# Respacing ScalarE's shrink work and the transform steps around TensorE's products

## The chip, the cores and the metric

The kernel runs on one core of a Trainium2 chip. The metric is device time in microseconds (us) of one execution; lower is better. Before the change the median was 2817.23 us (2814.24 to 2818.3).

## The reference

Two blocks, joined by a reshape, all in f32. The first multiplies a spectrum by a filter; the second is a feed-forward block whose nonlinearity is x − tanh(x):

```python
def _attn_ref(x, filt_r, filt_i):                 # x: 8 x 3008 x 256
    Y = np.fft.rfft(x, axis=1) * (filt_r + 1j * filt_i)[None, :, :]
    return np.fft.irfft(Y, n=x.shape[1], axis=1)

def _moe_ref(x, w_in, w_out):                     # x: 24064 x 256, d_ff = 2048
    h = x @ w_in
    g = h - np.tanh(h)
    return g @ w_out
```

## The kernel before

TensorE does nearly all the arithmetic. The eight sequences are worked in five batches: a single one, three pairs, a single one (in the code `UNITS = [(0,), (1, 2), (3, 4), (5, 6), (7,)]`). A batch has groups of tokens (6, 12, 12, 12, 6), a group has four **units**; 192 units in all. A unit's code interleaves four streams: `up` (the first product of the feed-forward block, as seven block products, here called P1 to P7), `shrink` of the unit before (x − tanh x), `down` of the unit before that (the second product, into the banks `o`; both `d()` and `e()` take its next piece), and **transform steps**, `t(0)` to `t(4)`, which do the spectral work of the *next* batch. In the last batch the steps are empty.

The `up` part, with cuts. `X`, `Y`, `Z` are banks of PSUM. P1, P6, P7, P4 all go into X, so X must be copied out before the next of them starts:

```python
def up(U, d, e, s, t):
    ...
    steps_at = ([1, 2, 0, 1, 0, 1, 1, 0] if U > 1 else [0, 0, 1, 0, 2, 0, 1, 2])
    ...                                   # shrinks(k) does steps_at[k] steps of shrink
    mm(X, 1, True)                        # P1
    mm(Y, 2, True)                        # P2
    s1 = copied("s1")                     # ScalarE copies X
    t(0); d(); shrinks(0)
    V.tensor_add(h[:, 0, :, 0:w], Y, s1)  # VectorE reads Y
    e(); shrinks(1)
    t(1)                                  # second transform step
    mm(X, 6, False)                       # P6
    mm(Z, 5, True)                        # P5
    u2 = copied("u2")
    shrinks(2); d(); shrinks(3); e()
    t(2)                                  # third
    mm(X, 7, False)                       # P7
    u3 = copied("u3")
    V.tensor_add(h[:, 3, :, 0:w], Z, u3)
    shrinks(4); d(); shrinks(5); e()
    t(3)                                  # fourth
    mm(X, 4, False)                       # P4
    V.tensor_copy(h[:, 2, :, 0:w], X)     # VectorE copies X; the next unit's P1 waits for it
    shrinks(6); d(); e()
    t(4)
    mm(Z, 3, False)                       # P3
    V.tensor_add(h[:, 1, :, 0:w], Z, u2)
    shrinks(7)
```

(Joined with semicolons here to save lines.) The shrink works on two halves of a unit's `h`, first half 2, then half 0. Per half there are three activations on ScalarE and two operations on VectorE: turn (arctan), power (a square, with a sum), the product h·y, square, and end:

```python
def start(k):
    ACT.activation(y[k], ht[k], AF.Arctan, scale=S)                    # turn
    ACT.activation(y[k], y[k], AF.Square, accum_out=y_sums[...])       # power
def square(k):
    V.tensor_mul(ht[k], ht[k], y[k])                                   # the product
    ACT.activation(sq[k], y[k], AF.Square, bias=near_b, scale=A)       # square
def end(k):
    V.scalar_tensor_tensor(out=ht[k], in0=sq[k], scalar=K, in1=ht[k], ...)

start(2); yield; square(2); yield; end(2); yield
start(0); yield; square(0); yield; end(0)
combine(...)                              # GpSimd sums for the second product
```

One kind of transform step, called `pz` after its tile, ends in this chain over four engines; a `pe` step of the same or a later unit reads its `uv`:

```python
ACT.mul(zs[0:IM], pz[IM:128], -1.0)       # L443
ACT.copy(zs[IM:128], pz[0:IM])            # L444
V.tensor_mul(rows(uv), rows(pz), fr)      # L445
G.tensor_mul(rows(zs), rows(zs), fi)      # L446, GpSimd
G.tensor_add(uv, uv, zs)                  # L447, GpSimd
```

Of the kernel before, what the change touches and what calls it, by code (L numbers as in the profile page):

```python
# [48 lines left out]
def chunks_of(unit, size):  # L49
    n = steps_of(unit)  # L50
    return [(r, min(size, n - r)) for r in range(0, n, size)]
# [92 lines left out]
def kernel(  # L144
# [10 lines left out]
    V, G, ACT = nc.vector, nc.gpsimd, nc.scalar  # L155
# [20 lines left out]
    groups = [(p, c) for p, bs in enumerate(UNITS) for c in range(len(chunks_of(bs, CH)))]  # L176
# [346 lines left out]
    def combine(b, t, shared=False):  # L523
        G.tensor_sub(t[0], b[0][1], b[0][0])  # L524
        G.tensor_sub(t[1], b[1][1], t[0])  # L525
        (V if shared else G).tensor_sub(t[2], b[1][1], b[0][1])  # L526
        G.tensor_sub(t[3], t[1], b[1][0])  # L527
# [4 lines left out]
    def up(U, d, e, s, t):  # L532

        i, u = divmod(U, 4)
        b, tu, w = uts[i]
        rhs = [b[0][0], b[1][0], b[1][1], tu[:, 3, 0:w], tu[:, 0, 0:w], tu[:, 1, 0:w],
               tu[:, 2, 0:w]]
        banks = {k: ps.tile([128, 2, 256], F32, tag=k, bufs=1, name=k) for k in "xyz"}
        X, Y, Z = (banks[k][:, :, 0:w] for k in "xyz")
        h = dn.tile([128, 4, 2, 256], F32, tag="h", bufs=3, name="h")  # L540
        hs[U] = (h, w)

        def mm(bank, q, first):
            for k in range(2):
                nc.tensor.matmul(bank[:, k], wu[:, q - 1, (2 * u + k) * 128:(2 * u + k + 1) * 128],  # L545
                                 rhs[q - 1], start=(first and k == 0), stop=True,
                                 skip_group_check=True)

        def copied(tag):
            t = dn.tile([128, 2, 256], F32, tag=tag, bufs=1, name=tag)[:, :, 0:w]  # L550
            ACT.copy(t, X)  # L551
            return t




        steps_at = ([1, 2, 0, 1, 0, 1, 1, 0] if U > 1 else [0, 0, 1, 0, 2, 0, 1, 2])

        def shrinks(at):
            for _ in range(steps_at[at]):  # L560
                s()

        mm(X, 1, True)
        mm(Y, 2, True)
        s1 = copied("s1")
        t(0)
        d()
        shrinks(0)
        V.tensor_add(h[:, 0, :, 0:w], Y, s1)  # L569
        e()  # L570
        shrinks(1)
        t(1)
        mm(X, 6, False)
        mm(Z, 5, True)
        u2 = copied("u2")
        shrinks(2)
        d()
        shrinks(3)
        e()
        t(2)  # L580
        mm(X, 7, False)
        u3 = copied("u3")
        V.tensor_add(h[:, 3, :, 0:w], Z, u3)  # L583
        shrinks(4)
        d()
        shrinks(5)
        e()
        t(3)
        mm(X, 4, False)
        V.tensor_copy(h[:, 2, :, 0:w], X)  # L590
        shrinks(6)
        d()
        e()
        t(4)
        mm(Z, 3, False)
        V.tensor_add(h[:, 1, :, 0:w], Z, u2)
        shrinks(7)

    def shrink(U):

        h, w = hs.pop(U)
        ht = {k: h[:, k:k + 2].rearrange("p a b n -> p (a b) n")[:, :, 0:w] for k in (0, 2)}

        def tiles(tag, bufs):
            return dn.tile([128, 4, 256], F32, tag=tag, bufs=bufs, name=tag)[:, :, 0:w]

        y, sq = {}, {}

        def start(k):
            y[k] = tiles("y", 2)  # L610
            ACT.activation(y[k], ht[k], AF.Arctan, scale=S)  # L611
            ACT.activation(y[k], y[k], AF.Square,  # L612
                           accum_out=y_sums[:, 2 * U + k // 2:2 * U + k // 2 + 1])

        def square(k):
            sq[k] = tiles("sq", 1)
            V.tensor_mul(ht[k], ht[k], y[k])  # L617
            ACT.activation(sq[k], y[k], AF.Square, bias=near_b, scale=A)  # L618

        def end(k):  # L620
            V.scalar_tensor_tensor(out=ht[k], in0=sq[k], scalar=K, in1=ht[k],  # L621
                                   op0=ALU.add, op1=ALU.mult)

        start(2)
        yield
        square(2)
        yield
        end(2)
        yield
        start(0)  # L630
        yield
        square(0)
        yield
        end(0)
        t = dn.tile([128, 4, 2, 256], F32, tag="t", bufs=2, name="t")
        blocks = [[h[:, 2 * a + k, :, 0:w] for k in range(2)] for a in range(2)]
        combine(blocks, [t[:, k, :, 0:w] for k in range(4)], U + 1 == 4 * len(groups))
        gs[U] = (blocks, t, w)
        yield
# [64 lines left out]
    def store(i, o):  # L704


        p, c = groups[i]
        r, n = CHUNKS[p][c]
        ws_ = widths(p, c)
        total = sum(ws_)  # L710
        ot = dn.tile([128, 2, CH * 128], F32, tag="ot", bufs=1, name="ot")
        for h in range(2):
            V.transpose(ot[:, h, 0:total], o[:, h, 0:total])
        b = UNITS[p][0]
        if len(UNITS[p]) == 2:
            blocks = [(r + 32 * q * NR, n, 32 * q) for q in range(4)]
        else:
            blocks = [(r_h + 32 * q * NR, n_h, rows.start + 32 * q)
                      for _, rows, r_h, n_h in halves(p, r, n) for q in range(2)]
        for h in range(2):  # L720
            for k in range(4):
                for row, m, lo in blocks:
                    outs.append((
                        dram(out.tensor, (b * SEQ + row) * DM + h * 128 + 32 * k,
                             [[NR * DM, 32], [DM, m], [1, 32]]),
                        ot[32 * k:32 * k + 32, h, :].rearrange(
                            "p (j c) -> p j c", c=128)[:, 0:m, lo:lo + 32]))
# [26 lines left out]
    def store_some(n):  # L754
        for dst, src in outs[:n]:
            nc.sync.dma_start(dst, src)
        del outs[:n]
# [81 lines left out]
    with tc.tile_pool(name="tr", bufs=2) as tr, tc.manual_schedule():  # L839
        with tc.tile_pool(name="pro", bufs=1) as pro, \  # L840
# [136 lines left out]
            for j in range(NK // 2):  # L977
# [7 lines left out]
                for i in range(2):  # L985
                    k = (2 * j + i) % 4
# [34 lines left out]
        with tc.tile_pool(name="dn", bufs=2) as dn, \  # L1021
# [48 lines left out]
            for U in range(total + 2):  # L1070
                i, u = divmod(U, 4)
                if U < total:
# [20 lines left out]
                    if u == 2 and i + 1 < len(groups):  # L1093
                        lasts = last(i + 1, z1)
                sh = shrink(U - 1) if 0 <= U - 1 < total else iter(())
                dw = down(U - 2) if 0 <= U - 2 < total else iter(())

                def d():

                    next(dw, None)  # L1100

                def e():

                    next(dw, None)

                def s():

                    next(sh, None)

                def t(k):  # L1110


                    nonlocal ms, done
                    quarter[0] = k
                    if k == 2 and stores:
                        store(*stores.pop())
                    store_some(4)
                    if U >= total:
                        return
                    pos = 20 * c + 5 * u + k  # L1120
                    if u == 3 and k in (0, 2) and i + 1 < len(groups):
                        next(lasts)
                    elif done < len(steps) and steps[done] <= pos:
                        if done < n_f:
                            next(fs)
                        else:
                            next(ms)
                        done += 1
                        if done == n_f:
                            ms = middle(p + 1, z1)  # L1130
                            next(ms)
                    next(late, None)
                    if U > 0 and k in (1, 3):
                        next(copies, None)

                if U < total:
                    if U == total - 1:
                        one = tr.tile([128, 128], F32, tag="x", bufs=3, name="one_sb")
                        nc.sync.dma_start(one, one_d)
                        ones = cst.tile([128, 1], F32, name="ones")  # L1140
                        G.memset(ones, 1.0)
                    up(U, d, e, s, t)
                else:
                    for k in range(5):
                        s()
                        s()
                        d()
                        e()
                        t(k)
                        if U == total + 1 and k == 0:  # L1150
                            bounded(z1)
# [39 lines left out]
```

## Time and profile before

| | before |
|---|---|
| median time | 2817.2 us |
| TensorE busy | 97% of the span, next VectorE with 68% |
| stops of TensorE, whole kernel | 124.0 us |
| of these ahead of the main loop | 54.5 |
| first batch / pairs 1, 2, 3 / last batch with tail | 25.1 / 10.9, 11.3, 12.1 / 10.0 |

A "stop" is not a row of the profile. It is worked out from the starts of the matmuls: what a start lies beyond the usual distance for its shape (216 ns for 128x256). Matmuls overlap in the records, so idle time of TensorE, as the page gives it, misses most of the short ones. All the sums of stops below are made this way from the trace.

In lines of the profile PE is TensorE, PEld its weight loads, DVE VectorE, ACT ScalarE, POOL GpSimd and SP SyncE; a trailing q is an engine's sequencer, and "issue" is time in which it waited for nothing that the profile shows. The prediction shows the page's busy line, the waits of the weight loads and three timelines. Beside them, the chain that ended last, read back from the final instruction, in shares of the span:

```profile
PE 79%; ACT 8%; DVE 4%; issue 4%; DMA 3%; POOL 2%; ACTq 0%; SPq 0%; DVEq 0%; POOLq 0%
```

### The profile page before, as it was taken

What the parts mean: (1) busy time and instruction counts of PE and PEld (TensorE: products, weight loads), DVE (VectorE), ACT (ScalarE), POOL (GpSimd) and SP (SyncE); (2) the same over time, 40 slices, a digit from 0 to 9 for tenths busy, and PEclk for the clock granted to TensorE, in tenths of its full rate; (3) what the DMA queues carried; (4) which work ended last, traced back from release to release, by engine and by line L of the source; (5) the groups of instructions that cost most, each with busy time, mean ns of one, the idle gap of its engine ahead of it and who ended that gap; (6) DMA issues with size and microseconds to landing.
All of it is one profiled execution on the core that took longest, in us unless ns stands there. A gap on an engine that the chain in (4) does not pass through costs nothing.

```text
span 2817.1 us, 36653 instructions
## 1 busy us (share of the span) xinstructions
PE 2725.6 (97%) x12438; PEld 2268.1 (81%) x12438; DVE 1913.8 (68%) x2175; ACT 1877.0 (67%) x2790; POOL 1796.2 (64%) x1407
## 2 busy tenths in 40 slices
PE   4899999999999999999999999999999999999998
PEld 2577777888878777888878887888888888898887
DVE  6755666666766676666677767666676777677776
ACT  2466776666667766666667776666666676666665
POOL 5546887544776767644576777755476666655555
PEclk7999999999999999999999999999999999999999
DMA  9854443332333322223323233112223322101010
GB/s 248 220 180 118 104 123 76 87 87 72 72 77 79 74 68 61 58 81 83 88 70 76 68 79 81 40 41 67 58 65 64 77 56 57 30 19 26 16 23 17
DMA packets 322592, 217.53 MB, mean 77 GB/s; under 512 B 224782, under 2 KB 274746, under 8 KB 322156
## 3 DMA queue, kind: packets, MB, share of 16 engines
q1 hardware_dynamic: 266826, 157.28, 24.0%
q10 hardware_dynamic: 52818, 51.53, 6.0%
q0 software_dynamic: 2752, 6.30, 0.8%
q8 instruction: 100, 1.64, 0.3%
q14 instruction: 96, 0.79, 0.1%
HBM read 138.87 MB, written 79.17 MB: 77 GB/s over the span
## 4 chain that ended last, share of the span: by engine, by line
PE 79%; ACT 8%; DVE 4%; issue 4%; DMA 3%; POOL 2%; ACTq 0%; SPq 0%; DVEq 0%; POOLq 0%
PE o L663 32%; PE x L545 20%; PE z L545 9%; PE y L545 5%; PE pe L411 3%; PE pu L511 3%; PE pz L430 3%; ACT y L611 2%; PE pf L351 2%; ACT u L551 1%; DVE h L617 1%; ACT zs L444 1%; ACT zs L443 1%; ACT y L612 1%; DVE h L590 1%
## 5 line engine op out<-in xcount | busy, mean ns | idle before, releaser
L663 PE MATMUL o<-t,wd 128*128 128x256 f32 (+2 forms) x3072 | 776.0, 375 | 1.8 <-POOL t L526 1.3
L617 DVE TENSOR_TENSOR h<-h,y 128x1024 f32<-128x1024 f32 (+2 forms) x384 | 572.4, 1491 | 275.8 <-ACT y L612 275.8
L663 PEld LDWEIGHTS o<-t,wd 128*128 128x128 f32 x3072 | 580.4, 190 | 74.1 <-POOL t L526 1.6
L545 PE MATMUL x<-tu,wu 128*128 128x256 f32 (+2 forms) x2304 | 587.6, 377 | 10.8 <-ACT u L551 10.5
L663 PE MATMUL o<-h,wd 128*128 128x256 f32 (+2 forms) x2304 | 582.3, 375 | 0.4 <-DVE h L621 0.4
L621 DVE SCALAR_TENSOR_TENSOR h<-sq,h 128x1024 f32<-128x1024 f32 (+2 forms) x384 | 567.5, 1478 | 20.6 <-ACT y L611 0.5
L524 POOL TENSOR_TENSOR t<-h 128x512 f32<-128x512 f32 (+2 forms) x192 | 240.1, 1250 | 503.7 <-DVE h L621 451.9
L545 PEld LDWEIGHTS x<-tu,wu 128*128 128x128 f32 x2304 | 426.3, 190 | 154.0 <-issue 68.9
L663 PEld LDWEIGHTS o<-h,wd 128*128 128x128 f32 x2304 | 431.1, 190 | 71.9 <-issue 18.4
L618 ACT ACTIVATE sq<-y,near_b 128x1024 f32<-128x1024 f32 (+2 forms) x384 | 435.6, 1134 | 5.0 <-DVE h L621 0.2
L611 ACT ACTIVATE y<-h 128x1024 f32<-128x1024 f32 (+2 forms) x384 | 400.0, 1042 | 15.7 <-ACT e L414 8.0
L612 ACT ACTIVATE y<-y 128x1024 f32<-128x1024 f32 (+2 forms) x384 | 399.2, 1040 | 12.2
L551 ACT COPY s<-x 128x512 f32<-128x512 f32 (+2 forms) x192 | 110.7, 577 | 441.6 <-PE x L545 433.0
L527 POOL TENSOR_TENSOR t<-t,h 128x512 f32<-128x512 f32 (+2 forms) x192 | 309.2, 1610 | 0.1
L551 ACT COPY u<-x 128x512 f32<-128x512 f32 (+2 forms) x384 | 218.9, 570 | 56.8 <-PE x L545 20.3
L525 POOL TENSOR_TENSOR t<-h,t 128x512 f32<-128x512 f32 (+2 forms) x192 | 240.8, 1254 | 15.1
L583 DVE TENSOR_TENSOR h<-z,u 128x512 f32<-128x512 f32 (+2 forms) x192 | 129.5, 674 | 176.8 <-ACT u L551 173.9
L526 POOL TENSOR_TENSOR t<-h 128x512 f32<-128x512 f32 (+2 forms) x191 | 248.0, 1298 | 0.0
L446 POOL TENSOR_TENSOR zs<-zs,ft 128x512 f32<-128x512 f32 x112 | 168.6, 1505 | 91.8 <-ACT zs L444 91.7
L447 POOL TENSOR_TENSOR uv<-uv,zs 128x512 f32<-128x512 f32 x112 | 210.7, 1881 | 15.6 <-DVE uv L445 7.2
L545 PE MATMUL x<-ut,wu 128*128 128x256 f32 (+2 forms) x768 | 198.7, 381 | 8.4 <-DVE h L590 4.8
L569 DVE TENSOR_TENSOR h<-y,s 128x512 f32<-128x512 f32 (+2 forms) x192 | 130.3, 679 | 102.0 <-PE y L545 89.1
(122 smaller groups left out, 3383.7 us busy)
## 6 DMA issues: line engine op xcount, KB each, us to landing
a<-ct SPq DMA_DIRECT2D x64, 384.0 KB, 4.0
ft<-filt SPq DMA_DIRECT2D x96, 256.0 KB, 4.7
out_dram<-ot SPq DMA_DIRECT2D x1392, 16.0 KB, 1.5
ct<-e ACTq DMA_DIRECT2D x112, 192.0 KB, 2.3
ct<-a ACTq DMA_DIRECT2D x80, 256.0 KB, 2.9
x_sb<-in_x_dram SPq DMA_DIRECT2D x69, 256.0 KB, 2.8
e<-ct SPq DMA_DIRECT2D x33, 512.0 KB, 4.5
fg<-fg SPq DMA_DIRECT2D x40, 392.0 KB, 6.2
```

Of the source, the lines that this page charges most:

```text
L524: G.tensor_sub(t[0], b[0][1], b[0][0])
L525: G.tensor_sub(t[1], b[1][1], t[0])
L526: (V if shared else G).tensor_sub(t[2], b[1][1], b[0][1])
L527: G.tensor_sub(t[3], t[1], b[1][0])
L545: nc.tensor.matmul(bank[:, k], wu[:, q - 1, (2 * u + k) * 128:(2 * u + k + 1) * 128], rhs[q - 1], start=(first and k == 0), stop=True, ski ...
L551: ACT.copy(t, X)
L611: ACT.activation(y[k], ht[k], AF.Arctan, scale=S)
L612: ACT.activation(y[k], y[k], AF.Square, accum_out=y_sums[:, 2 * U + k // 2:2 * U + k // 2 + 1])
L617: V.tensor_mul(ht[k], ht[k], y[k])
L618: ACT.activation(sq[k], y[k], AF.Square, bias=near_b, scale=A)
L621: V.scalar_tensor_tensor(out=ht[k], in0=sq[k], scalar=K, in1=ht[k], op0=ALU.add, op1=ALU.mult)
L663: nc.tensor.matmul(product(q), wd[:, q - 1, (2 * u + k) * 128: (2 * u + k + 1) * 128], rhs[q - 1][:, k], start=(u == 0 and k == 0 and q == ...
```

## The change

The change moves instructions and adds none. The three activations of a half no longer stand together: the shrink work between two copies of X on ScalarE is about the same each time. In the first batch the second transform step comes behind P6. In the pairs (where there are steps) the fourth comes behind P4 and the copy of X, so that VectorE copies X before it takes up the step's product. `close` is true in the first batch.

```diff
-        steps_at = ([1, 2, 0, 1, 0, 1, 1, 0] if U > 1 else [0, 0, 1, 0, 2, 0, 1, 2])
+        steps_at = ([1, 1, 1, 1, 0, 1, 1, 0] if U > 1 else [0, 0, 1, 0, 2, 0, 2, 1])
+        close = groups[i][0] == 0
...
-        t(1)
+        if not close:
+            t(1)
         mm(X, 6, False)
+        if close:
+            t(1)
...
-        t(3)
+        if close:
+            t(3)
         mm(X, 4, False)
         V.tensor_copy(h[:, 2, :, 0:w], X)
+        if not close:
+            t(3)
         shrinks(6)
...
-        start(2)
+        turn(2)
+        power(2)
+        yield
+        times(2)
         yield
         square(2)
+        turn(0)
         yield
         end(2)
         yield
-        start(0)
-        yield
+        power(0)
+        times(0)
         square(0)
         yield
         end(0)
```

(`start` is split into `turn` and `power`; the product leaves `square` and becomes `times`.)

More of the change, by code (lines that the diff above doesn't have):

```diff
@@ L607, in shrink, with turn, power, times @@
         y, sq = {}, {}
-        def start(k):
+        def turn(k):
             y[k] = tiles("y", 2)
             ACT.activation(y[k], ht[k], AF.Arctan, scale=S)
+        def power(k):
             ACT.activation(y[k], y[k], AF.Square,
                            accum_out=y_sums[:, 2 * U + k // 2:2 * U + k // 2 + 1])
+        def times(k):
+            V.tensor_mul(ht[k], ht[k], y[k])
         def square(k):
             sq[k] = tiles("sq", 1)
-            V.tensor_mul(ht[k], ht[k], y[k])
             ACT.activation(sq[k], y[k], AF.Square, bias=near_b, scale=A)
```

## The prediction

> **What bounds the kernel now.** I read the page first: busy shares, then the slices.
>
> ```profile
> PE 2725.6 (97%) x12438; PEld 2268.1 (81%) x12438; DVE 1913.8 (68%) x2175; ACT 1877.0 (67%) x2790; POOL 1796.2 (64%) x1407
> ...
> PE   4899999999999999999999999999999999999998
> ```
>
> TensorE (PE) is busy from the third slice to the end and no other engine passes 68%. All that order can win is time in which TensorE stands still, and 97% hides most of it: a matmul record of 128x256 lasts 379 ns, but the next starts 216 ns after it, so short stops vanish under the overlap. I therefore took all 12,438 starts and compared each distance with the median of its shape (216 ns for 128x256, 433 ns for 128x512, 112 ns for 128x128). What exceeds it is 124 us in all: 54.5 us before the first product of the main loop (at 122 us), then, per batch of groups, 25.1 (first, single; 24 units), 10.9, 11.3 and 12.1 (pairs; 48 units each), 10.0 (last, single, with the tail). So the loop loses 69 us, and the most that any reordering can give is about 2.5% of the time.
>
> The waits of the weight loads, which stand in front of the matmuls, name the causes:
>
> ```profile
> PEld x L545 <- ACT u L551: 34.5, 73, 1.9
> PEld x L545 <- DVE h L590: 24.1, 49, 2.2
> ...
> PEld pe L411 <- POOL uv L447: 4.5, 2, 3.3
> PEld pe L411 <- POOL t L525: 4.3, 3, 1.4
> ```
>
> (Columns: waiter, releaser, us, times, longest.) A unit of the loop puts P1, P6, P7, P4 into the one bank X; before each, the bank must be copied out: s1, u2, u3 by ScalarE, the last by VectorE (L590). By place, the 31.5 us lost in X in the three pair batches are: P4 waiting for u3, 5.3+5.4+1.8 = 12.5; P7 waiting for u2, 1.1+1.1+3.1 = 5.3; the next P1 waiting for L590, 3.9+4.3+5.5 = 13.7. The timeline shows a P4 stop:
>
> ```profile
> 792.53 1.06 ACT L612 ACTIVATE y<-y 128x1024 f32<-128x1024 f32 x1
> ...
> 793.71 0.59 ACT L443 ACTIVATE zs<-pz 64x512 f32<-64x512 f32 x1
> 794.32 0.58 ACT L444 COPY zs<-pz 64x512 f32<-64x512 f32 x1
> 794.91 0.58 ACT L551 COPY u<-x 128x512 f32<-128x512 f32 x1
> ...
> 795.55 0.73 PEld L545 LDWEIGHTS x<-tu,wu 128*128 128x128 f32 x4 [0.68 <-ACT u L551]
> ```
>
> ScalarE runs without a gap: two activations, the transform's two copies, then u3, late by 0.45 us. And a P1 stop:
>
> ```profile
> 1076.52 0.58 ACT L444 COPY zs<-pz 64x512 f32<-64x512 f32 x1
> ...
> 1077.19 0.69 DVE L445 TENSOR_TENSOR uv<-pz,ft 128x512 f32<-128x512 f32 x1 [1.05 <-ACT zs L444]
> ...
> 1077.79 0.68 DVE L590 COPY h<-x 128x512 f32<-128x512 f32 x1
> ...
> 1078.53 0.73 PEld L545 LDWEIGHTS x<-ut,wu 128*128 128x128 f32 x4 [0.52 <-DVE h L590]
> ```
>
> The fourth transform step's product (L445) waits for ScalarE's copies, and L590, queued behind it, waits too. In the first batch the repeating stop is `pe` in the second step:
>
> ```profile
> 313.75 0.69 DVE L445 TENSOR_TENSOR uv<-pz,ft 128x512 f32<-128x512 f32 x1 [3.02 <-ACT zs L444]
> ...
> 314.36 0.68 DVE L569 TENSOR_TENSOR h<-y,s 128x512 f32<-128x512 f32 x1
> ...
> 315.19 1.07 PE L411 MATMUL pe<-uv,fg 112*96 112x512 f32 x2 [1.08 <-POOL t L526]
> ```
>
> `pe` takes over bank Y and must wait until L569 has read it (its end, 315.04, is just before `pe` starts); GpSimd is named only because it ended something last. It costs 1.28 us in each of six units (10, 12, ... 20), in all 7.6.
>
> **What the Trainium skill says.** "Perfetto Trace Analysis", Identifying the Most-Contended Engine, says that matmul occupancy is a poor measure of how close one is to the roofline because matmuls are pipelined; the trace agrees (379 ns records at 216 ns distance). "TensorE: Matmul & The Clock Gate", "Wait — 56ns, not 53.3ns?", measures 215.7 ns between warm matmuls of 512 columns; here 216 ns is the floor, reached wherever nothing waits, so only stops can be saved. The same page, "What's actually happening", has the array fall to half clock after an idle window of about 3.4 us; in unit 8 (246 us) a 3.0 us stop is followed by eight matmuls at about double distance, 1.7 us more. "PSUM — Partial Sum Buffer", on bank collisions, says that any two engines on one bank and quadrant have to be kept apart, reads against reads too: that is why L445 waits for L444, though both only read `pz`.
>
> **The change, part by part.** No instruction is added or removed; the built programs have the same number on each engine. ScalarE's order was s1, turn2, power2, square2, (step 2), u2, turn0, power0, (step 3), u3, square0. It becomes s1, turn2, power2, (step 2), u2, square2, turn0, (step 3), u3, power0, square0. With 1.06 us for turn and power, 0.1 more for power's sum, 1.15 for square, the shrink work between the copies goes from 3.4 / 2.2 / 1.15 us to 2.2 / 2.2 / 2.3.
>
> P7 and P4. From P1's end to P6's end TensorE needs P2 0.86 + eight `o` 1.73 + P6 0.86 = 3.45 us; ScalarE before: s1 0.58 + 3.4 = 4.0, so u2 begins late (5.03 us after the unit's start in a clean unit, P6 ending at 4.48) and passes the delay on to u3. After: 0.58 + 2.2 = 2.8, u2 is on time. To P7's end again 3.45 us of TensorE, 0.58 + 2.2 = 2.8 of ScalarE. A step adds 0.86 to TensorE and at most 1.17 to ScalarE, which the spare 0.6 covers. The P7 stops should nearly end (5.3 to 0.5). For unit 44, whose P4 stop is shown above, the same sums give u3 finished 10.6 us after the unit's start, with P4 due at 11.3. P4 12.5 to 1, although the fourth step no longer stands between P7 and P4 (u3 needs 0.6 of the 1.73 left). Sum -16.3.
>
> P1, pairs. With the step behind L590, the stops after a `pz` in the fourth step go: 3.5+3.5+1.6 = 8.6. Against that, mul0 (L617) on VectorE now needs power0, which follows u3. In a clean unit with `down`'s last reads, mul0 begins 1.7 us after P7's end instead of 1.3, and L590 ends 2.6 us later: 4.3 against P1 due at 4.15, where there was 0.28 to spare. With the usual 0.1 us restart about 0.3 us, in some 12 such units (index 1 modulo 4, no step three or four) of the pairs: +3.6. Units with a store's transposes, some 10 at 0.1 to 0.2: +1. Net -4. One pair `pz` then `pe` a batch in one bank moves closer: +1.
>
> First batch. The second step moves behind P6 (0.86 us): 1.28 becomes some 0.4, six times: -5.3. In unit 1, two parts of the shrink leave VectorE's queue before L590: -1.3. P4 -0.6; part of unit 8's half clock -1; later L590 +0.7. Net -7.5.
>
> Last batch: no steps, so only mul0's lateness: five units at 0.3, five at 0.1: +2.
>
> Sum: -16.3 - 4 + 1 - 7.5 + 2 = -24.8 us. These stops are on TensorE, the chain itself, so they count one to one; but each start moved earlier can meet another wait that I have not listed, so I keep four fifths: -20, and 2817.2 becomes 2797 us.
>
> **Rivals.** (1) mul0's wait for power0 takes the place of the waits removed. For it: VectorE already waits 275.8 us for power (L617 on L612), and P1 had only 0.28 us spare in step-free units. Against it: most pair units have a third or fourth step behind P7, which gives 0.86 us more. If mul0 is also slowed beside GpSimd (1.2 us alone, up to 2.2 us in this trace), P1 loses 0.5 us in some 50 units and the gain is nearly gone: 2815. (2) The fourth step behind L590 delays the second half's end (L621) and the next unit's `o`, which waits for it; I get 6.7 us after P7 against `o` due at 6.7, or 7.6 where a step precedes it, as in nearly all these units. If wrong, half a us in 23 units: 2806. (3) Everything fits, and the stops of pairs and first batch vanish but for a few: 2787. (4) The floor is elsewhere (DMA, GpSimd): DMA is at two to three tenths in the loop and GpSimd at 64%; I give it nothing.
>
> **Range and chances.** The end of rival 3 and most of rival 1: 2786 to 2812. Faster by over 2% needs -56 us, four fifths of all the loop loses; 1%. Slower by over 2% would need new stops of 0.3 us at every unit above the old; 1%.
>
> **What would show it.** Right: the distances between TensorE starts lose about 20 us; L545's wait for u (34.5) falls under 12; no `pz`-then-P1 stop; `pe` stops in units 10 to 20 near 0.4 us. Wrong: the weight loads' wait for L590 (24.1) grows, with mul0 just before L590 on VectorE; or `o` waits for L621; or P4 still waits for u3 behind square2 and turn0.

## The result and the profile after

The changed kernel took 2805.61 us (median; 2803.72 to 2812.24) against 2817.15 us of the kernel before in the same rounds. The ratio is 0.9964, 95% interval 0.9951 to 0.9976. Ratios here are the mean time of one kernel's runs over that of the other's of the same rounds, so not quite the ratio of the medians. So the change wins 11 us. The prediction said 2797; its range, 2786 to 2812, held the result, but the gain was a little over half of what it named.

The lines of the page that answer to those of before, then the chain:

```profile
PE 2715.9 (97%) x12438; PEld 2273.4 (81%) x12438; DVE 1912.5 (68%) x2175; ACT 1885.6 (67%) x2790; POOL 1767.5 (63%) x1407
...
PE   4799999999999999999999999999999999999998
```

```profile
PE 83%; DVE 5%; ACT 4%; DMA 3%; POOL 2%; issue 2%; ACTq 0%; SPq 0%; DVEq 0%; POOLq 0%
```

The busy line says nothing: the work is the same and 97% stays 97%. The chain says more. ScalarE's share has halved, 8% to 4%; VectorE's has grown from 4% to 5%. The waits of the weight loads say which (waiter, releaser, us in total, times, longest; L596 is the copy of X that was L590, L633 the shrink's end that was L621):

```profile
PEld x L545 <- DVE h L596: 26.5, 46, 1.3
...
PEld o L680 <- DVE h L633: 11.3, 21, 2.6
...
PEld x L545 <- ACT u L551: 3.0, 4, 1.9
```

The wait for ScalarE's copies went from 34.5 us to 3.0. The wait for VectorE's copy of X did not shrink but rose, 24.1 to 26.5, although its largest known cause was taken away. And `o` now waits for the shrink's end: 11.3 us, where the page of before has 1.9.

The stops of TensorE, worked out as above, in us:

| | ahead of loop | first batch | pair 1 | pair 2 | pair 3 | last, tail | sum |
|---|---|---|---|---|---|---|---|
| before | 54.5 | 25.1 | 10.9 | 11.3 | 12.1 | 10.0 | 124.0 |
| after | 57.4 | 19.1 | 6.6 | 6.6 | 11.0 | 9.7 | 110.5 |

Ahead of the loop nothing was changed; the other profiles have 53.9 to 56.9 there, so that is run-to-run. The loop lost 16.4 us of stops. In the three pair batches, by the matmul that was late:

| pairs | P4 | P7 | P1 | `o` | `pe` | other |
|---|---|---|---|---|---|---|
| before | 12.5 | 5.3 | 13.7 | 0 | 1.2 | 1.6 |
| after | 0.7 | 0 | 16.3 | 3.4 | 2.8 | 1.0 |

Now the three places that the prediction showed. First unit 44, with the P4 stop (timeline; start, us, engine, line, operation):

```profile
787.67 0.59 ACT L443 ACTIVATE zs<-pz 64x512 f32<-64x512 f32 x1 [0.41 <-PE pz L430]
...
788.28 0.58 ACT L444 COPY zs<-pz 64x512 f32<-64x512 f32 x1
788.88 0.58 ACT L551 COPY u<-x 128x512 f32<-128x512 f32 x1
...
790.00 1.03 PE L545 MATMUL x<-tu,wu 128*128 128x256 f32 x4
```

ScalarE now has time to wait for `pz` (0.41 us idle ahead of L443). u3 ends at 789.46, half a microsecond before P4 starts at 790.00, and nothing is put down as a wait. Second, the end of unit 63, with the P1 stop behind a `pz` of the fourth step:

```profile
1067.93 0.68 DVE L596 COPY h<-x 128x512 f32<-128x512 f32 x1
...
1069.41 0.69 DVE L445 TENSOR_TENSOR uv<-pz,ft 128x512 f32<-128x512 f32 x1 [0.81 <-ACT zs L444]
...
1069.61 1.03 PE L545 MATMUL x<-ut,wu 128*128 128x256 f32 x4
```

The copy of X now comes ahead of L445 and ends 1.0 us before P1 (1069.61) starts. Third, unit 12 in the first batch:

```profile
315.27 0.68 DVE L571 TENSOR_TENSOR h<-y,s 128x512 f32<-128x512 f32 x1
...
316.10 1.07 PE L411 MATMUL pe<-uv,fg 112*96 112x512 f32 x2 [0.21 <-DVE h L571]
```

`pe` still waits for L571 to read Y, but with P6 ahead of it only 0.42 us are lost (by the starts) in place of 1.28. In each of the three the change did what it was meant to do.

### The profile page after: what moved, and what is told of

Read it like the earlier page. It is cut to its first block, busy times and chain, and to the rows that moved or that the text cites. A ratio compares the mean times of both kernels' runs of the same rounds, so it can differ in the third digit from the quotient of the medians.

```text
span 2803.4 us, 36463 instructions
## 1 busy us (share of the span) xinstructions
PE 2715.9 (97%) x12438; PEld 2273.4 (81%) x12438; DVE 1912.5 (68%) x2175; ACT 1885.6 (67%) x2790; POOL 1767.5 (63%) x1407
## 4 chain that ended last, share of the span: by engine, by line
PE 83%; DVE 5%; ACT 4%; DMA 3%; POOL 2%; issue 2%; ACTq 0%; SPq 0%; DVEq 0%; POOLq 0%
PE o L680 35%; PE x L545 21%; PE z L545 10%; PE y L545 5%; PE pe L411 3%; PE pz L430 3%; PE pu L511 3%; PE pf L351 2%; DVE h L626 2%; ACT y L622 1%; DVE h L596 1%; DMA raw<-in_moe_w_in_dram 1%; DMA filt<-in_filt_r_dram 1%; ACT y L619 1%; DVE h L633 0%
## 5 line engine op out<-in xcount | busy, mean ns | idle before, releaser
L626 DVE TENSOR_TENSOR h<-h,y 128x1024 f32<-128x1024 f32 (+2 forms) x384 | 577.4, 1504 | 311.5 <-ACT y L622 310.4
L633 DVE SCALAR_TENSOR_TENSOR h<-sq,h 128x1024 f32<-128x1024 f32 (+2 forms) x384 | 558.7, 1455 | 121.0 <-ACT sq L630 113.0
L527 POOL TENSOR_TENSOR t<-t,h 128x512 f32<-128x512 f32 (+2 forms) x192 | 318.9, 1661 | 0.1
L447 POOL TENSOR_TENSOR uv<-uv,zs 128x512 f32<-128x512 f32 x112 | 206.7, 1846 | 9.1 <-DVE uv L445 0.5
L545 PE MATMUL z<-tu,wu 128*128 128x256 f32 (+2 forms) x768 | 194.5, 376 | 0.0
```

The source lines that it names most:

```text
L527: G.tensor_sub(t[3], t[1], b[1][0])
L545: nc.tensor.matmul(bank[:, k], wu[:, q - 1, (2 * u + k) * 128:(2 * u + k + 1) * 128], rhs[q - 1], start=(first and k == 0), stop=True, ski ...
```

## The experiments

"Alone" is one part of the change on the kernel before; the others are edits of the changed kernel. All were correct.

### The shrink's spacing alone

The changed kernel with both moved steps put back:

```diff
-        if not close:
-            t(1)
+        t(1)
         mm(X, 6, False)
-        if close:
-            t(1)
...
-        if close:
-            t(3)
+        t(3)
         mm(X, 4, False)
         V.tensor_copy(h[:, 2, :, 0:w], X)
-        if not close:
-            t(3)
```

> Only the shrink's new split and places; the second and fourth transform steps stand where they stood before. My theory: the stops of P4 and P7 in the pair batches go as in the changed kernel (17.8 us before, 0.7 after), but the product of the first half now waits for its power behind u3, and with the fourth step still before the copy of X the stops of P1 grow, from 13.7 us to about 27 in the pairs (8.6 us of stops behind pz stay and each lengthens by some 0.3 us, and the clean units gain 0.3 us each). Net about -2 us: 2815. Rival (ScalarE's balance is the whole gain, the places of the steps hardly matter): 2806, as the whole change.

Measured: 2817.21 us, ratio 0.9998 (0.9984 to 1.0011). The P4 and P7 stops of the pairs fall from 17.8 us to 0.8, as in the whole change, and the P1 stops rise from 13.7 to 27.4. So this part removes what it was aimed at and pays nearly all of it back at P1: in the pairs it is worth −3.7 us. Two things grow. Most stops behind a `pz` of the fourth step, 0.27 to 0.39 us each before, are now 0.51 to 0.57. And there are new stops of up to 0.9 us, of which more below.

### The second step alone

```diff
+        close = groups[i][0] == 0
-        t(1)
+        if not close:
+            t(1)
         mm(X, 6, False)
+        if close:
+            t(1)
```

> Only the second transform step behind P6 in the first batch; shrink and fourth step as before. My theory: six pe stops fall from 1.28 to about 0.4 us (-5 us), the start of the loop loses some of it again: 2813, with the pair batches unchanged to 0.5 us. Rival (the first batch's gain came from the shrink): 2817.

Measured: 2814.55 us, ratio 0.9987 (0.9973 to 1.0001). First-batch stops 25.1 to 19.3 us, most of it at `pe` (12.0 to 7.8); the pairs don't move. The trace shows the 6 us, the clock 3. (Some 1.7 of the 6 us are a stretch at half clock in unit 8, which the profile of before has and this one has not; it hangs on luck too, see below, on the first batch.)

### The fourth step alone

```diff
-        t(3)
+        if close:
+            t(3)
         mm(X, 4, False)
         V.tensor_copy(h[:, 2, :, 0:w], X)
+        if not close:
+            t(3)
```

> Only the fourth step behind P4's copy in the pairs; shrink as before. My theory: the stops of P1 behind pz go (8.6 us), P4 gains at most 3 us where u3 is over 1 us late, and since the first half's product is early, no new wait of o for the half's end: 2810. Rival (the shift itself causes the new waits of o, 3.4 us in the pairs): 2813 with stops of o of over 2 us in the third pair batch.

Measured: 2818.3 us, ratio 1.0002 (0.9988 to 1.0016). My expectation fell here and the rival was right. P1 stops of the pairs fall by 7.2 us, to 6.5, but P4 comes 2.0 later (12.5 to 14.5: no step stands between P7 and P4 any more to hide the late u3), `o` stops 3.8 us for the shrink's end, and `pe` 1.6 more.

Against the 2817.28 us of the kernel before in those rounds, the parts alone give −0.1, −2.7 and +1.0, in sum −1.8 us; whole, the change is worth 11. In the pairs, by stops: −3.7 and +0.4 alone, −10.1 together. The clock's intervals would not carry this alone; the stops do. Each of the two parts cures what the other brings: the spacing gets u3 ready early, which the moved fourth step needs, and the moved step takes the `pz` copies out of P1's way, which the spacing had made later.

### The product behind the copy of X

This tests whether it is the product of half 0, ahead of the copy of X, that makes P1 late. It becomes a step of its own, behind the copy, everywhere:

```diff
-        steps_at = ([1, 1, 1, 1, 0, 1, 1, 0] if U > 1 else [0, 0, 1, 0, 2, 0, 2, 1])
+        steps_at = ([1, 1, 1, 1, 0, 1, 1, 1] if U > 1 else [0, 0, 1, 0, 2, 0, 2, 2])
...
         V.tensor_copy(h[:, 2, :, 0:w], X)
+        shrinks(6)
         if not close:
             t(3)
-        shrinks(6)
+        shrinks(7)
...
-        shrinks(7)
...
         power(0)
-        times(0)
         square(0)
         yield
+        times(0)
+        yield
         end(0)
```

> The whole change, but the first half's product h*y on VectorE stands behind the copy of X after P4 (and before the fourth step) rather than in front of it, so that the copy no longer waits for a product that waits for power. My theory (this wait gave back what the change won): the stops of P1 fall from 16.3 us in the pairs and 2.6 us in the last batch to under 5 in all; stops of o behind the half's end may gain 2 to 4 us; time about 2795. Rival (P1 is then held by something else, or the later end of the half stops o as much): 2804 or more.

Measured: 2801.59 us, ratio 0.9945 (0.9931 to 0.9958). P1's stops in the pairs go from 16.3 us to 0, which settles the place. It isn't free even there: `o`, which waits for the shrink's end, stops for 6.9 us in the pairs in place of 3.4. The time was missed by 6.6, because the first batch, where steps stand closer, pays: its stops are 28.4 us against 19.1 (`pe` 11.9, most of it put down to GpSimd's addition for `uv`; `o` 6.3, most of it put down to the shrink's end); some 2 us of the batch's stops are a stretch at half clock in unit 8.

### The changed kernel again, and the product moved in the pairs only

```diff
+    def behind(U):
+        return U < 4 * len(groups) and len(UNITS[groups[U // 4][0]]) == 2
...
         V.tensor_copy(h[:, 2, :, 0:w], X)
+        if behind(U):
+            shrinks(6)
         if not close:
             t(3)
-        shrinks(6)
+        shrinks(7 if behind(U) else 6)
...
-        times(0)
+        if not behind(U + 1):
+            times(0)
         square(0)
         yield
+        if behind(U + 1):
+            times(0)
+            yield
         end(0)
```

> The changed kernel once more, on the chip of the three kernels that follow, so that they can be compared with it: 2805 to 2806.

> The first half's product behind the copy of X in the pair batches alone; first and last batch as in the changed kernel. My theory: the pair batches lose 12.4 us as in the kernel with the product behind the copy everywhere (24.2 us in the changed kernel), the first 19 and the last 10: 12 us less than the changed kernel, 2794. Rival (the first batch's 9 us of new stops came from elsewhere, or what the pairs give is lost at the next batch): 2800 or more.

Measured in the same rounds: the changed kernel unaltered 2806.44 us, ratio 0.9964 (0.995 to 0.9977); with the product moved in the pairs 2794.04 us, ratio 0.992 (0.9907 to 0.9934), as expected. Stops of the pairs: 6.7, 6.5, 11.0 for the one and 3.4, 3.5, 5.7 for the other, 11.6 us less, and the medians differ by 12.4. So P1's wait behind the product is worth about as much as the whole change had won.

### The second step moved from the third unit on only

The first two units of the kernel are cold: there the moved step leaves nothing to fill P6's wait for GpSimd's sums (2.45 us of stop in unit 0). This leaves the step ahead of P6 for them, alone and together with the edit above:

```diff
-        if not close:
+        if not close or U < 2:
             t(1)
         mm(X, 6, False)
-        if close:
+        if close and U > 1:
             t(1)
```

> The changed kernel with the second transform step behind P6 only from the third unit on. In the first unit P6 waits for GpSimd's sums for 2.4 us and the step behind it can no longer fill that time; the idle array then runs eight matmuls at about half clock. My theory: 2.5 us less than the changed kernel, 2803. Rival (that start is hidden behind the weights or the first products of the shrink anyway, as the stop of o in unit 2 takes it up): 2805.5.

> Both of these: the gains add, 2791.5, if they touch different stretches; 2794 if the second is worth nothing.

Measured: 2804.17 us, ratio 0.9961 (0.9948 to 0.9975) alone; 2792.23 us, ratio 0.9918 (0.9905 to 0.9932) with both. Against their partners without this edit (0.9964 and 0.992) neither is told apart. In the trace, P6 stops in the first batch fall from 2.3 us to 0.3 and `pf`, another transform product, rises by 1, so that unit 0 stops for 4.25 us in place of 5.32. But the first batch's sum is 19.1 with and 18.7 without, because unit 8, whose code is the same in both and which waits for 3.32 us in both, went on at half clock in the one profile (1.7 us more, most of it counted at `o`) and at full clock in the other. What the edit is worth, about 1 us, is less than this luck. The kernel with both edits is the fastest measured here, by a margin over the one before that means nothing.

### GpSimd's addition in two halves

What remained was *why* the product made P1 so late. Of the nine largest P1 stops of the pairs, eight lie where a `pz` stands in the third step: units 44, 45, 66, 92, 93, 114, 156, 158, with 6.6 us of stops at the P1 that follows, 0.7 to 0.9 each. (The ninth is unit 121, 1.19 us, of which 0.74 stood before; a `pf` is in its third step.) In unit 156, before and after (timeline, VectorE's product L617 or L626, GpSimd's addition L447, and the copy of X):

```profile
2354.94 1.22 DVE L617 TENSOR_TENSOR h<-h,y 128x1024 f32<-128x1024 f32 x1
2355.12 2.16 POOL L447 TENSOR_TENSOR uv<-uv,zs 128x512 f32<-128x512 f32 x1
...
2356.07 0.68 DVE L590 COPY h<-x 128x512 f32<-128x512 f32 x1
```

```profile
2340.69 1.27 POOL L447 TENSOR_TENSOR uv<-uv,zs 128x512 f32<-128x512 f32 x1
...
2340.95 2.10 DVE L626 TENSOR_TENSOR h<-h,y 128x1024 f32<-128x1024 f32 x1 [0.36 <-ACT y L622]
...
2342.97 0.68 DVE L596 COPY h<-x 128x512 f32<-128x512 f32 x1
...
2343.70 1.13 PE L545 MATMUL x<-ut,wu 128*128 128x256 f32 x4 [0.54 <-DVE h L596]
```

Before, the product starts first (by 0.18 us) and takes 1.22 us; the addition takes 2.16, and ends 1.12 us after the product. After, the product has waited 0.36 us for power and starts 0.26 us behind the addition; now the addition takes 1.27 us and the product 2.10, of which 1.01 pass before the addition ends (2341.96). Whoever starts second stands still until the first is done. The page "SBUF — State Buffer" of the Trainium skill, Who interferes with whom, says that VectorE shares a port pair with GpSimd, that a VectorE instruction with two SBUF inputs contends with a GpSimd instruction that reads SBUF, and that "Issue order, not op shape, decides who blocks." The trace agrees in both orders. The addition starts 0.28 us after P4 (2354.84 and 2340.41) in both kernels; the product went from 0.18 us ahead of it to 0.26 us behind it, 0.44 us later. But the copy of X, behind the product, ends 3.24 us after P4's start (2343.65 − 2340.41) in place of 1.91 (2356.75 − 2354.84): 1.33 us later, the 0.44 us and the 0.88 us by which the product is longer. Before, P1 started at 2357.43, 0.68 us after the copy's end. The delay alone would have fitted into that; delay and block together do not.

The block by itself makes no stop. Units 46, 56, 94 and 104 also have a `pz` in the third step, and their product takes 2.09 to 2.20 us, but P1 was due 3.45 us after P4, the copy of X ended at 3.23 to 3.34, and P1 stopped for 0.05 us at most. In units 46 and 94 the product was as long before the change. In unit 136 the product still came first.

There is a control in the kernel before: in unit 158 a store's transposes made the product start 0.04 us behind the addition already, it took 2.31 us, and the P1 that follows stopped for 0.81 us, before as after.

If the lock is held for one instruction, two shorter instructions must let VectorE in between:

```diff
-            G.tensor_add(uv, uv, zs)
+            for part in (slice(0, w // 2), slice(w // 2, w)):
+                G.tensor_add(uv[:, :, part], uv[:, :, part], zs[:, :, part])
```

> The changed kernel with GpSimd's addition uv+zs split into two halves of columns. Theory: in the eight pair units with a pz in the third step (44, 45, 66, 92, 93, 114, 156, 158) the product h*y of VectorE, 0.44 us later than before, now starts after this addition has started and is blocked until it ends (product 2.1 us instead of 1.2). If the hold lasts one instruction, halving it frees VectorE after the first half: the product ends some 0.4 to 0.6 us earlier, the P1 stops of the third-step units in the pairs (6.6 us, of 16.3 in all) fall by about 4, and 2806 becomes about 2802, perhaps 2803 with the added instruction. Rival: the product is long because both engines share bandwidth all the time, or GpSimd's two halves hold VectorE one after the other; then the product stays near 2.1 us and the time stays at 2806, or rises by what GpSimd's extra instruction delays pe and e.

> The best kernel so far (product behind the copy of X in the pairs, second step moved from the third group on; 2792) with the same split. There the product is no longer before the copy of X, so the blocked product is off TensorE's path: the theory expects no gain, 2792 within 2, or 1 to 2 more if the extra GpSimd instruction makes pe later. The rival, that GpSimd's length itself is what counts somewhere, would show 2789 or less, or a clear loss.

Measured: 2801.75 us, ratio 0.9946 (0.9933 to 0.996), on the changed kernel; 2794.15 us, ratio 0.9911 (0.9895 to 0.9926), on the fastest one, where the product is out of P1's way. Unit 156 with the split (all lines one further down):

```profile
2336.09 2.39 POOL L448 TENSOR_TENSOR uv<-uv,zs 128x256 f32<-128x256 f32 x2
...
2336.34 1.56 DVE L627 TENSOR_TENSOR h<-h,y 128x1024 f32<-128x1024 f32 x1 [0.35 <-ACT y L623]
...
2337.82 0.68 DVE L597 COPY h<-x 128x512 f32<-128x512 f32 x1
```

The product starts 0.25 us behind the addition, as before the split, but takes 1.56 us in place of 2.10. The two halves of the addition together span 2.39 us, and end 0.58 us after the product: the second half now waits in its turn. Stops at the eight P1s: 6.6 us to 2.7, P1 stops of the pairs 16.3 to 12.8. The intervals of the two ratios (0.9964 and 0.9946) overlap and the runs were on different chips, so the clock alone would not carry it; the three pair batches in the trace are 1982.0 us and 1979.1 us long, 2.9 less. Where the product is behind the copy, the split brings nothing, as expected. ("Third group" in that text means the third unit.) The rival, bandwidth shared all along, would have left the product near 2.1 us, and falls; nor would it fit that whichever of the two came first kept its short time (1.22 us, 1.27 us).

## Why the prediction was right, and where it was off

The point was 8.6 us too low. By its own steps, in stops:

| step of the prediction | predicted | measured |
|---|---|---|
| P7 and P4 in the pairs | −16.3 | −17.1 |
| P1 in the pairs | −4 | +2.6 |
| `pz`, then `pe`, in one bank | +1 | +1.6 |
| `o` in the pairs | 0 (rival 2) | +3.4 |
| first batch | −7.5 | −6.0 |
| last batch | +2 | −0.3 |
| other stops in the pairs | – | −0.6 |
| sum | −24.8 | −16.4 |

**P7 and P4** were right in size and in mechanism: the wait for u fell to 3.0, against a bound of 12 named beforehand. Of the signs named for "wrong", two came: the wait for the copy of X grew, and `o` waits for the shrink's end.

**P1** is the step that failed, by a term that was left out. Its parts that were worked out held. The copy of X no longer waits behind L445, and of the 8.6 us of stops behind a `pz` of the fourth step, 1.1 are left (units 54, 65, 102, 113, where L445 now follows the copy too): there a store's transposes or sums of `down`, with the product, come ahead of the copy. In a unit of index 1 modulo 4 without a step, the copy of X ends 4.32 us after P7, predicted 4.3, and six such units stop for 0.32 us, predicted 0.3 in some 12. Units with a store's transposes (index 2 modulo 4) cost more than the 1 us allotted: the nine stops of 0.32 to 0.55 us behind them, some of which stood before, are 2.3 us more in all. But the sentence "most pair units have a third or fourth step behind P7, which gives 0.86 us more", used against the first rival, was wrong for a third step. It stands ahead of P7, so it gives nothing behind it: in unit 156 P1 was due 4.15 us after P7's end, as in a unit without a step. And where it is a `pz`, it starts GpSimd's addition just ahead of the product, which loses the order to it. These eight stops make 6.6 us, of which 0.8 stood before (unit 158); with the 1.3 us too little for the stores' units, that is the gap in this row, less a few tenths. The rival's second half ("if mul0 is also slowed beside GpSimd") was the true cause, with the right size for one product, up to 2.2 us; it was weighed for some 50 units, made P1 stop in eight, and was then given nothing. The experiment with the split shows the lock, and the one with the product behind the copy shows the place; that the shrink's spacing alone brings these eight stops and the moved step alone does not (of the eight, 0.33, 0.32 and the old 0.81 us stop there) shows which part of the change they belong to.

**`o`**: rival 2 came true in six units (64, 112, 136, 144, 146, 148), each behind a unit with a `pz` in the fourth step, and with no step of its own ahead of `o`. The prediction gave the time right, 6.7 us against `o` due at 6.7, and leaned on "in nearly all these units" a step precedes; it holds in most of its 23 units and not in six. Unit 64:

```profile
1070.02 1.73 DVE L633 SCALAR_TENSOR_TENSOR h<-sq,h 128x1024 f32<-128x1024 f32 x1
...
1070.75 2.14 POOL L447 TENSOR_TENSOR uv<-uv,zs 128x512 f32<-128x512 f32 x1
...
1071.81 1.13 PE L680 MATMUL o<-h,wd 128*128 128x256 f32 x4 [0.31 <-DVE h L633]
```

The end of the shrink (L633), behind L445 on VectorE, is done at 1071.75 and `o` starts at 1071.81. It stopped for 0.47 us, with 0.10 more at the next start, as after most stops in these traces.

**First batch**: the six `pe` stops are 0.42 us, predicted 0.4. Unit 1's gain is there too (2.06 to 0.73 us at the P1 that follows, predicted −1.3), but the `o` right behind it took it back, 0.47 to 2.01 us, which was not foreseen. Nor was unit 0, where P6, with its neighbours, lost 2.5 us, over 1 us of it at half clock. Against that, unit 8's half clock vanished (1.7 us, 1 predicted). That was luck: its wait grew (3.03 to 3.48 us), both kernels with the second step moved from the third unit on, with the same code there, have the half clock in unit 8, and the kernel with the fourth step alone, with the code of before there, has not.

**Last batch**: P1's new stops are 1.5 us, predicted 2; that `o` had 1.5 less is no effect of the change that I could show, since it was 3.8 in one profile of the changed kernel and 5.5 in the other, and up to 6.9 in kernels with the same order for this stretch.

The share "four fifths" that was kept for waits not listed turned −24.8 into −20. By stops the loop kept two thirds, 16.4; the medians show 11.5, of which the profile's own span (2817.1 to 2803.4, with 2.9 us more ahead of the loop) accounts for 13.7. The last few us between stops and clock lie within the spread of runs and are left open. One comparison of the prediction needs care: the 215.7 ns that it sets beside 216 ns belong to 512 columns, but in this trace 216 ns is the distance of a 128x256 record, and 128x512 takes 433. The floor rests on this trace alone.

## What to carry to other kernels

When an instruction is moved later on VectorE, look not only at what waits for it but at what GpSimd starts in that instant: a few tenths of a microsecond can exchange which of the two stands still, and the penalty is then what is left of the other's instruction (here 1.01 us), on top of the delay. A kernel at 97% busy still has stops to win, but two parts of a reordering can be worth nothing alone and 10 us together, so test them together and apart. And if an operation needs something late, put it behind the copy that frees a bank, where the schedule has room for its result: in the pairs that was worth as much again as the change, and in the first batch, where there was no room, it cost.

## What the Trainium skill lacked or had wrong

- "SBUF — State Buffer": nothing lacking or wrong on this point. For a VectorE instruction with two SBUF inputs its summary table has the second one to issue blocked until the first finishes. The runs agree in both orders (product 1.22 us first and addition 2.16; addition 1.27 first and product 2.10), and with the addition in two halves the product takes 1.56 us.
- "TensorE: Matmul & The Clock Gate", What's actually happening: it names a free-running idle window of about 3.4 us, after which the array falls to half clock. In the twelve traces the granted clock changes only at multiples of 3.41 us from one another, which agrees. But a window need not be idle throughout: between 110 and 2700 us all eight windows with 2.00 us or more of idle time (by the records' ends, which are modelled) were followed by half clock, and no window with 1.98 or less was, from full clock. So how long one idle stretch is does not decide: 2.18 us (unit 0 after) fell into one window and brought half clock; 3.32 us (unit 8 after) was split, 1.98 and 1.34, and brought none.
- The cost of starting again, which no page that I read gives: after most stops in these traces the second matmul, too, starts 104 ns later than its usual 216 ns.
